# Fewer half-width batches at the end of an attention and soft-MoE kernel, and the last expert's products added to the spreading product

## Chip, cores and metric

One core of a Trainium2 chip runs the whole kernel. The metric is the device time in microseconds, as the median of several runs. The time before the change is 178.54 us (three runs, 178.18 to 178.70).

## What is computed

The reference is attention over 8 batches, 8 heads, 576 positions and 64 dimensions, followed by a mixture of 8 experts with 4 slots each. Heads 0 to 3 see a window of 32 positions, heads 4 to 7 every fourth position of a window of 128.

```python
x = attention(q, k, v)            # 4608 rows of 512
logits = x @ phi                  # 512 x 32 slots
d = softmax(logits, axis=0)       # over the rows
slot_input = (d.T @ x).reshape(8, 4, 512)
for e in range(8):
    h = np.maximum(slot_input[e] @ w1[e], 0.0)     # 512 x 1024
    slot_out[e] = h @ w2[e]                        # 1024 x 512
c = softmax(logits, axis=1)       # over the slots
return c @ slot_out               # 4608 x 512
```

The output is fp32; the kernel computes in fp16 with fp32 sums. The inputs are 62 MB and the output 9.4 MB in HBM.

## The kernel before

**First part.** A software pipeline over the 8 batches (the order of its steps is written out by hand in `ORDER`) computes the attention, the logits and their exponentials `ET`, and sums up the slots' inputs in `U`. All instructions of an engine run in the order in which the program names them (`tc.manual_schedule()`).

**Loads.** POOL issues every load of q, k, v, w1 and w2, with a cast from fp32 to fp16, into one queue that 16 transfer engines work off in order. The loads of the weights are spread between those of the batches. The last ones are issued when the buffers of the last batches come free (line 549 on): `load_full(late, 2, 3, 6)` brings w2 of experts 3, 4 and 5 in one transfer into the tile `late`; then `load_half` brings w2 of experts 6 and 7 in column halves: the left 256 columns of 6 (one transfer) and 7 (two transfers, of four of the eight row chunks each), then the right 256 columns likewise.

**The experts.** After the last batch, the slots' inputs are normalized and transposed (`siTm`), multiplied by w1 (line 608), passed through the ReLU into `h_sb`, transposed (line 618) and copied to `hTm` (lines 620 and 623). `hTm[:, g, c, 32*j : 32*j+32]` holds the hidden values of expert 4g+j for chunk c of the 1,024 hidden units, as 32 columns of which only the four of that expert's slots aren't zero. `emit_so` (line 641) multiplies them by w2 into `so`, a PSUM tile of 128 rows. The products of experts 0 to 3 use the row groups by expert, those of the others by c modulo 4, so four run side by side on the array, and each of the four groups of 32 rows of `so` ends up with a part of the sum.

**Gather and spread.** `gather_so(s)` copies one half (s = 0 left, 1 right; `DH` = 256 columns) of `so` to fp16 on DVE (`so_part`, line 652). `spread_so(s)` multiplies it by a constant matrix `spread`, which adds the four parts and puts the sum into all four groups of 32 rows (`rep`, line 657), and ACT copies that to `so_sb` (line 658).

**Output.** `emit_batch(b, c0, c1)` makes 512 rows of batch b in the columns c0 to c1: four products of `ET` with `so_sb` (line 664, PSUM tiles `f`, four buffers), each scaled and copied to `om[b]` by ACT and DVE in turn (lines 673 and 677), and then one store that POOL issues (line 686; batch 0's left half goes in two stores). The first `NHALF` = 6 batches are made in two passes, left halves first. Between the left halves stand expert 6's right-half products (ahead of batch 2), expert 7's (ahead of batch 4) and the gather of the right half (ahead of batch 5); the spreading of the right half comes behind batch 5. Batches 6 and 7 are made in full width, and the last 64 positions of all batches (`om_l`, line 713) end it.

Of the kernel before, what the change touches and what calls it, by code (L numbers as in the profile page):

```python
# [9 lines left out]
FP32 = mybir.dt.float32  # L10
FP16 = mybir.dt.float16
# [29 lines left out]
DH = DMODEL // 2  # L41
# [55 lines left out]
def kernel(  # L97
# [10 lines left out]
    nc = tc.nc  # L108
# [10 lines left out]
    spread = cst[:, o + 128 : o + 256]  # L119
# [10 lines left out]
    so_part = consts.tile([128, DMODEL], FP16, name="so_part")  # L130
    so_sb = consts.tile([128, DMODEL], FP16, name="so_sb")
    hTm = consts.tile([128, 2, 8, 128], FP16, name="hTm")
# [3 lines left out]
    w1t, w2t = {}, {}  # L136

    def weights_tile(pool, which, e0, e1):
        n = (4 * FDIM, 8 * DMODEL)[which - 1]
        t = pool.tile([128, e1 - e0, n], FP16, name=f"w{which}_{e0}", tag=f"w{which}_{e0}")  # L140
        for e in range(e0, e1):
            of = t[:, e - e0]
            if which == 1:
                w1t[e] = of.rearrange("p (c f) -> p c f", c=4)
            else:
                w2t[e] = of.rearrange("p (c n) -> p c n", c=8)
        return t
# [16 lines left out]
    def slab_weights(e, tag, n):  # L164
        t = fix.tile([128, n], FP16, name=f"w2_{e}", tag=tag)
        w2t[e] = t[:, 0 : 8 * DMODEL].rearrange("p (c n) -> p c n", c=8)
# [9 lines left out]
    ring = ctx.enter_context(tc.tile_pool(name="ring", bufs=2, space=bass.MemoryType.PSUM))  # L176
# [28 lines left out]
    def load_full(t, which, e0, e1):  # L205
        if which == 1:
            nc.gpsimd.dma_start(
                out=t.rearrange("p e (u x) -> p (e u) x", u=2),
                in_=moe_w1[e0:e1].rearrange("e (u p c) f -> p (e u) (c f)", u=2, p=128),
            )  # L210
        else:
            nc.gpsimd.dma_start(
                out=t, in_=moe_w2[e0:e1].rearrange("e (p c) n -> p e (c n)", p=128)
            )

    def load_half(e, s, n):
        src = moe_w2[e].rearrange("(p c) n -> p c n", p=128)
        cols = slice(DH * s, DH * s + DH)
        for u in range(0, 8, n):
            nc.gpsimd.dma_start(out=w2t[e][:, u : u + n, cols], in_=src[:, u : u + n, cols])  # L220
# [249 lines left out]
    for which in "QK":  # L470
        load_raw(which, 1)
    nc.gpsimd.dma_start(
        out=phi_raw.rearrange("p (u c) s -> p u (c s)", u=2),
        in_=moe_phi.rearrange("(u p c) s -> p u (c s)", u=2, c=2),
# [15 lines left out]
    def step(op, b):  # L490
        if op[0] in "ARM" and op[1:] in TILES:
            kind, i = TILES[op[1:]]
            if op[0] == "A":
                tmp[(op[1:], b)] = emit_av(b, kind, i)
            elif op[0] == "R":
                tmp[("R" + op[1:], b)] = emit_recip(b, kind, i, tmp[(op[1:], b)])
            else:
                engine = nc.scalar if op[1:] in ON_ACT else nc.vector
                norm_mult(b, kind, i, tmp.pop((op[1:], b)), tmp.pop(("R" + op[1:], b)), engine)
        elif op in ("S0", "S1", "S2"):  # L500
            tmp[(op, b)] = emit_scores(b, int(op[1]))
        elif op in ("E0", "E1", "E2"):
            emit_exp(b, int(op[1]), tmp.pop(("S" + op[1], b)))
        elif op in ("MK0", "MK1", "MK2"):
            emit_mask(b, int(op[2]))
        elif op[0:2] in ("QT", "KT", "VT"):
            turn(op[0], b, int(op[2]))
        elif op in ("XP0", "XP1"):
            tmp[(op, b)] = xT_plain(b, int(op[2]))
        elif op in ("XD0", "XD1"):  # L510
            tmp[(op, b)] = xT_dil(b, int(op[2]))
        elif op in ("XPc0", "XPc1", "XDc0", "XDc1"):
            xT_copy(b, op[1], int(op[3]), tmp.pop((op[0:2] + op[3], b)))
        elif op in ("VA", "VB", "VC", "VD"):
            tmp[(op, b)] = v_rows(b, "ABCD".index(op[1]))
        elif op in ("VAc", "VBc", "VCc", "VDc"):
            v_place(b, "ABCD".index(op[1]), tmp.pop((op[0:2], b)))
        elif op in ("LG", "EP"):
            tmp[(op, b)] = (back_logits if op == "LG" else back_erow)(b)
        elif op == "ET":  # L520
            back_et(b, tmp.pop(("LG", b)))
        elif op == "ER":
            back_er(b, tmp.pop(("EP", b)))
        else:
            {"ED": back_erd, "U": back_u, "UT": back_add}[op](b)

    def loads(which, b):
        load_raw(which, b)
        if which == "V":
            if b > 2:  # L530
                load_weights(1)
            if b == B - 1:
                load_weights(len(weights))
# [5 lines left out]
    w2b_pool = None  # L539
    for it in range(B + max(s for _, s in STEPS)):  # L540
        for op, stage in STEPS:
            b = it - stage
            if not 0 <= b < B:
                continue
            step(op, b)
            if op in frees and b + 2 < B:
                loads(frees[op], b + 2)
            left.discard((op, b))
            if w2b_pool is None and not left:
                raw_pool.release()  # L550
                w2b_pool = tc.alloc_tile_pool(name="w2b", bufs=1, side="right")
                late = weights_tile(w2b_pool, 2, 3, 6)
                slab_weights(6, "qk0", QK_SLAB)
                slab_weights(7, "qk1", QK_SLAB)
                load_full(late, 2, 3, 6)
                for s in range(2):
                    for e in (6, 7):
                        load_half(e, s, 8 if e == 6 else 4)
        if it == 0:
            nc.vector.tensor_copy(  # L560
                out=phi4, in_=phi_raw[:, :, None, :].broadcast_to([128, 4, 4, N_SLOTS])
            )
# [6 lines left out]
    h_pool = tc.alloc_tile_pool(name="hp", bufs=1)  # L569
# [33 lines left out]
    for fc in range(2):  # L603
        for g in range(2):
            for dc in range(4):
                for j in range(4):
                    e = 4 * g + j
# [4 lines left out]
                        start=(g == 0 and dc == 0),  # L612
                        stop=(g == 1 and dc == 3),
# [3 lines left out]
    for c in range(8):  # L617
# [3 lines left out]
        out=hTm[:, 0].rearrange("p c (j s) -> p c j s", j=4)[:, :, :, 0:16], in_=hT4[:, :, :, 0:16]  # L621
    )
    nc.scalar.copy(
        out=hTm[:, 1].rearrange("p c (j s) -> p c j s", j=4)[:, :, :, 16:32], in_=hT4[:, :, :, 16:32]
    )
    psum_e.release()
    psum_f = tc.alloc_tile_pool(name="psum_f", bufs=4, space=bass.MemoryType.PSUM)

# [6 lines left out]
    def emit_so(s, experts):  # L635
        cols = slice(0, DMODEL) if s is None else slice(DH * s, DH * s + DH)
        for c in range(8):
            for e in experts:
                g, j = divmod(e, 4)
                row = 32 * (j if len(experts) == 4 else c % 4)  # L640
                nc.tensor.matmul(
                    so[row : row + 32, cols],
                    hTm[:, g, c, 32 * j : 32 * j + 32],
                    w2t[e][:, c, cols],
                    start=(e < 4 and c == 0),
                    stop=(e == 7 and c > 3),
                    skip_group_check=True,
                )

    def gather_so(s):  # L650
        cols = slice(DH * s, DH * s + DH)
        nc.vector.tensor_copy(out=so_part[:, cols], in_=so[:, cols])

    def spread_so(s):
        cols = slice(DH * s, DH * s + DH)
        rep = ring.tile([128, DH], FP32, name=f"rep_{s}", tag="ring")
        nc.tensor.matmul(rep, spread, so_part[:, cols], start=True, stop=True)
        nc.scalar.copy(out=so_sb[:, cols], in_=rep)

    turn = [0]  # L660

# [25 lines left out]
                out=dst[:, j0 : j0 + n, c0:c1], in_=om[b][:, j0 : j0 + n, c0:c1]  # L687
            )

    NHALF = 6  # L690
    emit_so(None, (0, 1, 2, 3))
    for e in (4, 5):
        emit_so(None, (e,))
    for e in (6, 7):
        emit_so(0, (e,))
    gather_so(0)
    spread_so(0)
    for b in range(NHALF):
        if b in (2, 4):
            emit_so(1, ({2: 6, 4: 7}[b],))  # L700
        if b == 5:
            gather_so(1)
        emit_batch(b, 0, DH, 2 if b == 0 else 4)
    spread_so(1)
    for b in range(NHALF):
        emit_batch(b, DH, DMODEL)
    for b in range(NHALF, B):
        emit_batch(b, 0, DMODEL)
# [3 lines left out]
    for e in range(2):  # L712
        nc.gpsimd.dma_start(
            out=rest[:, e, 512:576, :].rearrange("n i d -> i n d"), in_=om_l[64 * e : 64 * e + 64]
# [37 lines left out]
```

## Time and profile before

| | |
|---|---|
| profiled execution | 178.29 us |
| its span, first to last instruction | 176.5 us |
| mean granted TensorE clock | 0.87 |
| PE / DVE / ACT / POOL busy | 70% / 71% / 70% / 22% |
| last product, last eviction | 165.0, 165.8 us |
| last output transfer issued, last one landed | 167.0, 175.2 us |

All times within the execution are microseconds from the start of the span. PE is the matrix engine (TensorE), PEld its weight loads, DVE the vector engine, ACT the scalar engine; POOL issues the transfers. In groups and timelines, `L664` is a line of the kernel, `f<-so_sb,ET` says what is written from what, and the brackets say how long the engine was idle before and what ended that. A chain line has a start, a length and the work in it. A window line has its limits and length, the busy time and the number of instructions of PE, PEld, DVE, ACT and POOL, the granted clock, the mean busy share of the 16 transfer engines (over 1 where an engine has two packets under way), and GB/s. A transfer line has the number of issues, the size in KB and the median time from issue to landing. Where the text gives the landing of a single transfer, it is the last of its 16 completion counts in the trace, one from each transfer engine.

### The profile page before, as it was taken

To read this page: it belongs to the slowest core of one execution; us is meant where nothing else is said; L and a number is where in the kernel's file an instruction comes from. 1 tells how busy PE (TensorE), PEld (TensorE's weight loads), DVE (VectorE), ACT (ScalarE), POOL (GpSimd) and SP (SyncE) were. 2 spreads that over 40 slices of the span, in tenths; PEclk is the share of its full clock that TensorE was granted. 3 is DMA by queue.
4 is the path that set the end of the run, shared out by engine and by line. 5 is a ranking of instruction groups with operands and counts; after the bars stand their busy time and mean duration, and the time that the engine had idled before them with its cause. 6 is when DMAs were issued, how large, how long until landed. Compare 5 with 4: busy or idle time off the path is not lost.

```text
span 176.5 us, 4724 instructions
## 1 busy us (share of the span) xinstructions
PE 123.5 (70%) x2004; PEld 80.9 (46%) x2004; DVE 126.0 (71%) x275; ACT 123.5 (70%) x266; POOL 38.4 (22%) x60
## 2 busy tenths in 40 slices
PE   0026928998888888988989888978677295778300
PEld 0015616676566566656766557656332142221000
DVE  6473899999999999999999998465130104878500
ACT  6007758999999999999999999995501104888300
POOL 7321022112112112116000002710000001856600
PEclk9999999969999999999789999996858969655555
DMA  5999999999999999999999999999999999999997
GB/s 83 215 214 210 214 212 215 215 213 214 216 212 217 211 218 215 208 215 220 213 211 217 213 218 216 222 210 225 213 213 221 192 198 175 340 398 397 401 415 209
DMA packets 18981, 40.83 MB, mean 231 GB/s; under 512 B 1169, under 2 KB 11537, under 8 KB 18193
## 3 DMA queue, kind: packets, MB, share of 16 engines
q0 software_dynamic: 18816, 40.41, 113.8%
q8 instruction: 15, 0.25, 0.5%
q1 hardware_dynamic: 144, 0.14, 0.3%
q14 instruction: 6, 0.04, 0.1%
HBM read 62.07 MB, written 9.44 MB: 405 GB/s over the span
## 4 chain that ended last, share of the span: by engine, by line
ACT 38%; DMA 27%; DVE 14%; PE 10%; issue 2%; POOL 2%; POOLq 0%; ACTq 0%
DMA w<-in_moe_w_dram 19%; ACT p L282 10%; DMA phi_raw<-in_moe_phi_dram 8%; ACT vX L253 7%; ACT xp L337 7%; DVE qk L231 5%; PE f L664 5%; ACT om L673 3%; ACT xT L376 3%; ACT xT L378 3%; DVE p L293 3%; DVE vT L231 3%; ACT xd L337 2%; PE s L273 2%; PE rp L357 2%
## 5 line engine op out<-in xcount | busy, mean ns | idle before, releaser
L282 ACT ACTIVATE p<-s 128x1920 f16<-128x1920 f32 (+1 forms) x24 | 44.6, 1857 | 10.2 <-PE s L273 10.1
L273 PE MATMUL s<-qk 32*128 32x128 f16 (+2 forms) x704 | 26.7, 295 | 18.4 <-DVE qk L231 12.0
L253 ACT COPY vX<-rv 128x768 f16<-128x768 f16 (+1 forms) x32 | 27.8, 943 | 1.8 <-PE rv L247 1.8
L316 PEld LDWEIGHTS <-p 128*128 128x128 f16 (+1 forms) x480 | 22.4, 103 | 13.3 <-DVE xp L341 4.0
L337 ACT ACTIVATE xp<-o_P,rc_P 128x64 f16<-128x64 f32 x96 | 26.5, 497 | 2.2 <-DVE rc_P L328 2.2
L273 PEld LDWEIGHTS <-qk 32*128 32x128 f16 x704 | 17.3, 117 | 21.6 <-DVE qk L231 12.0
L293 DVE TENSOR_TENSOR p<-p,masks 128x1920 f16<-128x1920 f16 (+1 forms) x24 | 25.7, 1084 | 0.2
L231 DVE STREAM_TRANSPOSE qk<-rawQ 128x576 uint32<-128x576 uint32 x16 | 18.8, 1243 | 2.7 <-DMA rawQ<-in_q_dram 2.7
L316 PE MATMUL o_P<-vX,p 128*128 128x65 f16 (+1 forms) x288 | 20.0, 205 | 0.8 <-ACT xp L337 0.2
L231 DVE STREAM_TRANSPOSE qk<-rawK 128x576 uint32<-128x576 uint32 x16 | 19.5, 1231 | 0.4 <-DMA rawK<-in_k_dram 0.4
L247 PE MATMUL rv<-cst,vT 128*128 128x128 f16 x176 | 17.5, 242 | 3.2 <-DVE vT L231 1.8
L231 DVE STREAM_TRANSPOSE vT<-rawV 128x576 uint32<-128x576 uint32 x16 | 19.4, 1223 | 0.5 <-DMA rawV<-in_v_dram 0.5
L686 POOL DMA_DIRECT2D out_dram<-om x15 | 11.1, 744 | 39.2 <-DVE om L677 34.8
L247 PEld LDWEIGHTS <-vT 128*128 128x128 f16 x176 | 13.2, 124 | 7.5 <-issue 3.7
L677 DVE TENSOR_SCALAR om<-f,rrow 128x256 f16<-128x256 f32 (+1 forms) x28 | 13.5, 519 | 3.5 <-PE f L664 2.9
L664 PE MATMUL f<-so_sb,ET 32*128 32x256 f16 (+1 forms) x60 | 12.5, 392 | 3.9 <-ACT om L673 2.7
L673 ACT ACTIVATE om<-f,rrow 128x256 f16<-128x256 f32 (+1 forms) x28 | 12.8, 503 | 2.6 <-PE f L664 2.0
L376 ACT COPY xT<-rp 128x576 f16<-128x576 f16 x16 | 11.5, 909 | 1.3 <-PE rp L357 1.3
L316 PE MATMUL o_D<-vX,p 128*128 128x65 f16 x128 | 9.9, 202 | 2.5 <-DVE xp L341 2.0
L201 POOL DMA_DIRECT2D rawQ<-in_q_dram x8 | 5.1, 633 | 29.4 <-DVE rc_P L328 18.4
L378 ACT COPY xT<-rd 128x576 f16<-128x576 f16 x16 | 10.6, 795 | 0.0
L341 DVE TENSOR_TENSOR xd<-o_D,rc_D 128x256 f16<-128x256 f32 x24 | 9.9, 412 | 0.2
(81 smaller groups left out, 176.7 us busy)
## 6 DMA issues: line engine op xcount, KB each, us to landing
w<-in_moe_w_dram POOLq DMA_DIRECT2D x3, 3072.0 KB, 35.5
out_dram<-om POOLq DMA_DIRECT2D x11, 512.0 KB, 4.6
w<-in_moe_w_dram POOLq DMA_DIRECT2D x5, 1024.0 KB, 15.9
rawQ<-in_q_dram POOLq DMA_DIRECT2D x8, 576.0 KB, 12.7
rawK<-in_k_dram POOLq DMA_DIRECT2D x8, 576.0 KB, 11.4
rawV<-in_v_dram POOLq DMA_DIRECT2D x8, 576.0 KB, 11.6
out_dram<-om POOLq DMA_DIRECT2D x2, 1024.0 KB, 7.3
w<-in_moe_w_dram POOLq DMA_DIRECT2D x2, 512.0 KB, 36.7
```

The costliest lines, as they stand in the source:

```text
L231: nc.vector.transpose(out=out_, in_=in_)
L247: nc.tensor.transpose(rg[:, n_t, :, c, :], rows, ident)
L253: copy(out=vX[b % 2][:, t0 : t0 + n, :, 0:D], in_=rg.rearrange("p n h c d -> p n h (c d)"))
L273: nc.tensor.matmul(sps[:, h, c0 : c0 + w], kk, qq, start=(tt == 0), stop=(tt == 1))
L282: return nc.scalar.activation(out=pt, in_=sps[:, :, 0:n], func=AF.Exp, scale=SCALE)
L293: return nc.vector.tensor_tensor(out=pt, in0=pt, in1=m, op=ALU.mult)
L316: nc.tensor.matmul(o[rows, h, :], lhs, rhs, start=(n == 0), stop=(n == len(jobs) - 1), skip_group_check=True,)
L337: nc.scalar.activation(out=dst[:, h], in_=src[:, h], func=AF.Copy, scale=rc[:, h : h + 1])
L376: copy(out=xT_t[b][:, c, :], in_=rg[:, 0:S])
L378: copy(out=xT_t[b][:, 2 + c, :].rearrange("p (i r) -> p i r", r=DIL), in_=rg[:, :, 0:SUB].rearrange("p r i -> p i r"),)
L664: nc.tensor.matmul(fp[:, 0 : c1 - c0], ET[32 * j : 32 * j + 32, m : m + 128], so_sb[32 * j : 32 * j + 32, c0:c1], start=True, stop=True,)
L673: nc.scalar.activation(out=dst, in_=fp[:, 0 : c1 - c0], func=AF.Copy, scale=rrow[:, blk : blk + 1])
```

## The change

- `NHALF` is 4 instead of 6: batches 4 and 5 are made and stored in full width.
- Expert 7's products leave `so`. Its hidden values are copied on DVE into a new tile `hT7`, repeated four times side by side, and its products are 128 wide: they give the same 32 rows in all four groups. They are added in PSUM to the spreading product: `gather_so` now starts that product (`stop=False`) as soon as experts 0 to 6 are gathered, and `last_so` adds expert 7's eight products and copies the result to `so_sb`.
- Right half: expert 6's products, the gather and the spreading product stand ahead of batch 2, and `last_so(1)` behind batch 3.
- w2 of expert 3 gets its own tile and its own transfer, ahead of that of experts 4 and 5.

```diff
-                late = weights_tile(w2b_pool, 2, 3, 6)
+                late = {x: weights_tile(w2b_pool, 2, *x) for x in ((3, 4), (4, 6))}
 ...
-                load_full(late, 2, 3, 6)
+                for x, t in late.items():
+                    load_full(t, 2, *x)
 ...
+    hT7 = h_pool.tile([128, 8, 4, 32], FP16, name="hT7", tag="hT7")
+    nc.vector.tensor_copy(out=hT7, in_=hTm[:, 1, :, None, 96:128].broadcast_to([128, 8, 4, 32]))
 ...
-                    stop=(e == 7 and c > 3),
+                    stop=(e == 6 and c > 3),
 ...
+    rep = {}
     def gather_so(s):
         cols = slice(DH * s, DH * s + DH)
         nc.vector.tensor_copy(out=so_part[:, cols], in_=so[:, cols])
+        rep[s] = ring.tile([128, DH], FP32, name=f"rep_{s}", tag="ring")
+        nc.tensor.matmul(rep[s], spread, so_part[:, cols], start=True, stop=False)
 
-    def spread_so(s):
+    def last_so(s):
         cols = slice(DH * s, DH * s + DH)
-        rep = ring.tile([128, DH], FP32, name=f"rep_{s}", tag="ring")
-        nc.tensor.matmul(rep, spread, so_part[:, cols], start=True, stop=True)
-        nc.scalar.copy(out=so_sb[:, cols], in_=rep)
+        for c in range(8):
+            nc.tensor.matmul(
+                rep[s],
+                hT7[:, c].rearrange("p a s -> p (a s)"),
+                w2t[7][:, c, cols],
+                start=False,
+                stop=(c == 7),
+            )
+        nc.scalar.copy(out=so_sb[:, cols], in_=rep[s])
 ...
-    NHALF = 6
+    NHALF = 4
     emit_so(None, (0, 1, 2, 3))
     for e in (4, 5):
         emit_so(None, (e,))
-    for e in (6, 7):
-        emit_so(0, (e,))
+    emit_so(0, (6,))
     gather_so(0)
-    spread_so(0)
+    last_so(0)
     for b in range(NHALF):
-        if b in (2, 4):
-            emit_so(1, ({2: 6, 4: 7}[b],))
-        if b == 5:
+        if b == 2:
+            emit_so(1, (6,))
             gather_so(1)
         emit_batch(b, 0, DH, 2 if b == 0 else 4)
-    spread_so(1)
+        if b == 3:
+            last_so(1)
```

## The prediction

> **What bounds the kernel now.** I read the page's slices first, then the chain of waits, then the last 40 us: queue, engines, transfers.
>
> Page, part 2 (40 slices of 4.4 us):
>
> ```profile
> PEclk9999999969999999999789999996858969655555
> DMA  5999999999999999999999999999999999999997
> GB/s 83 215 214 210 214 212 215 215 213 214 216 212 217 211 218 215 208 215 220 213 211 217 213 218 216 222 210 225 213 213 221 192 198 175 340 398 397 401 415 209
> ```
>
> The transfer engines are busy from end to end: inputs at some 213 GB/s of fp16 landed, outputs at 400 GB/s of fp32. The dip to 175 GB/s is where loads end and outputs begin. The chain of waits, there:
>
> ```profile
> 112.33 34.05 DMA w<-in_moe_w_dram
> ...
> 146.76 0.43 DVE so_part L652
> 147.23 0.28 PE rep L657
> 147.54 0.38 ACT so_sb L658
> 147.96 0.31 PE f L664 x4
> ...
> 154.63 0.41 PE f L664 x4
> ```
>
> From the landing of expert 7's left half (146.37) to the first product of the output (147.96) lie 1.59 us of small steps; the right half's output products begin at 154.63. The chain leaves out that the transfer queue, one queue issued by POOL, drains until 175.2 while the engines are done at 165.8. In windows:
>
> ```profile
> 148.50:149.50 1.00, 0.71 (x8) 0.29 (x9) 1.00 (x3) 1.00 (x4) 0.10 (x1) 1.00 1.15 155
> 149.50:150.50 1.00, 0.89 (x13) 0.38 (x13) 0.79 (x3) 0.80 (x3) 1.00 (x2) 1.00 0.70 94
> 152.50:154.50 2.00, 1.16 (x6) 0.45 (x5) 1.96 (x5) 1.90 (x5) 1.29 (x2) 0.50 1.98 405
> 168.00:170.00 2.00, 0.00 (x0) 0.00 (x0) 0.00 (x0) 0.00 (x0) 0.00 (x0) 0.50 1.46 411
> ```
>
> The last two columns are DMA share and GB/s. There is a hole at 149 to 150.5, but not in every transfer engine: the 16 completions of the last load come between 149.0 and 151.70. The early engines wait for output, the latest goes straight on (its first output completes at 152.45). All 16 then write at one pace, and the latest at the loads' end is still about 0.6 us late at the end. So **the end is the latest engine's load end, 151.70, plus its output work, plus a tail**, as long as output is ready for it. POOL's issues and the transfers:
>
> ```profile
> 149.40 3.03 POOL L686 DMA_DIRECT2D out_dram<-om  x4 [33.97 <-DVE om L677]
> 155.06 0.75 POOL L686 DMA_DIRECT2D out_dram<-om  x1 [0.37 <-issue]
> 156.48 0.74 POOL L686 DMA_DIRECT2D out_dram<-om  x1 [0.67 <-ACT om L673]
> ...
> out_dram<-om POOLq DMA_DIRECT2D x11, 512.0 KB, 4.6
> out_dram<-om POOLq DMA_DIRECT2D x2, 1024.0 KB, 7.3
> out_dram<-om POOLq DMA_DIRECT2D x2, 256.0 KB, 3.0
> ```
>
> The issue at 149.40 has its first packet at 150.68: 1.28 us. Eleven half-width batches (512 KB) land from 153.14 to 167.69, 1.323 us each; the two full batches (1 MB) land at 170.18 and 172.73, 2.52 us each. The issue at 156.48 is the first right half; its landing, 161.06, less its own 1.32, less 0.3 that a landing lies behind its last packet, says that the queue came to it at 159.45. It could have started at 156.48 + 1.28 = 157.76: **1.7 us of slack**, worked out from these, not shown as a wait.
>
> **The change part by part.**
>
> *Two batches full instead of halved.* Four transfers of 1.323 become two of 2.52: 5.29 - 5.04 = **-0.25 us**, all on the queue that sets the end. Sixteen half-width evictions become eight full ones (0.47 against 0.69 us each on ACT): off the path, as the engines end 9 us before the queue.
>
> *w2 of expert 3 alone.* One more issue on POOL, 0.77 us, ahead of expert 6's at 106.34; the issues behind it wait until 111.58 anyway for a buffer, and land 30 us later. Hidden; without that backlog 0.77. On the queue it adds one completion: two 256 KB pieces land 0.69 apart, one 512 KB piece 1.32, so 2 x 0.69 - 1.32 = **+0.06**. What it lets go early:
>
> ```profile
> 138.44 0.40 PE L641 MATMUL so<-w,hTm 128*32 128x512 f16 x3 [0.52 <-DVE hTm L620]
> 141.15 4.61 PE L641 MATMUL so<-w,hTm 128*32 128x512 f16 x57 [2.31 <-DMA w<-in_moe_w_dram]
> ```
>
> Experts 0 to 3 (32 products) no longer wait for 141.15. They end by about 140.3, but nothing can end before expert 7 lands at 146.37; today PE is through with the rest at 145.76. Worth nothing by itself.
>
> *The copy to hT7.* 1,024 values a partition on DVE behind ACT's copy that ends at 139.0. The 512-value copy at L620 takes 0.42, so 0.4 to 0.9. DVE is idle until 146.76: nothing; without that cover, at most 0.9.
>
> *Expert 7, left half.* Gather (0.43), spreading (0.28) and their gaps leave the path behind the landing; in come four of eight 128-wide products (the first four have their weights at 145.04). Products of 512 columns start 0.213 apart at clock 1.0 and 0.427 at 0.5, so one of 256 costs 0.107 or 0.213, and four end at 147.0, or at 147.46 at half clock, against 147.50 for the spreading now. Output products begin 0.46 or 0.04 earlier. Which? Clock 1.0 in 144.3 to 151.1 follows a stretch (140.9 to 144.3) in which PE worked off the late experts 0 to 5. With 0 to 3 done earlier, that stretch holds some 1.1 us of work at full clock. I take half clock, 0.04. The Trainium skill, "TensorE: Matmul & The Clock Gate", Part 1, says that the array's clock is released by a busy window of about 3.4 us and falls back after an idle one; by that rule spending the products early speaks against this change. The trace bears it out in kind: the 3.4 us after the wait for 141.15 ran at 0.5. In either case the latest transfer engine gains nothing from an earlier first output, since it isn't waiting at 151.70.
>
> *Right half.* This is where it can cost. Now expert 6's and 7's products are slipped between batches 1/2 and 3/4, and the gather between batches 4/5. ACT's evictions:
>
> ```profile
> 148.26 1.67 ACT L673 ACTIVATE om<-f,rrow 128x256 f16<-128x256 f32 x4 [0.35 <-PE f L664]
> 150.13 1.72 ACT L673 ACTIVATE om<-f,rrow 128x256 f16<-128x256 f32 x4 [0.20 <-PE f L664]
> 152.51 1.77 ACT L673 ACTIVATE om<-f,rrow 128x256 f16<-128x256 f32 x4 [0.66 <-PE f L664]
> 155.04 5.62 ACT L673 ACTIVATE om<-f,rrow 128x256 f16<-128x256 f32 x12 [0.46 <-PE f L664]
> ```
>
> After the change: (a) the gather stands ahead of batch 2 on DVE, and the spreading on PE waits for it with batch 2's output products behind it. DVE is free of batch 1 at 150.03, gathers until 150.45, the spreading starts at 150.5, batch 2's first product ends at 150.9: ACT resumes at 150.94 where it resumed at 150.13, +0.8. (b) Batches 2 and 3 take 1.75 more: to 152.7. (c) PE starts the eight wide products at 152.05 (batch 3's last output product); at the clock of 0.5 that the trace shows there they take 8 x 0.213 = 1.7 us plus 0.15 to drain: 153.95. Expert 7's last quarter lands at 151.70, before its turn. Then the copy to so_sb, 0.37, and the first right-half product at 154.42. Today that is 154.63: **only 0.2 earlier, with two half batches (2.65 us of queue) fewer ahead of it**. So the slack of 1.7 becomes 1.7 + 0.2 - 2.65 = -0.75: the queue runs dry for **0.75 us**, even for its latest engine, just before the first right half. Bounds: at full clock in (c) and the 0.46 of earlier start, the slack stays positive: 0. With batches 0 to 2 at half clock as well (0.2 to 0.3 more) and no gain in (c): 1.0; if the next two right halves too come late (they have 0.35 us to spare, and today one of the gaps between issues there is 1.42), up to 2.0. I take 0.75, nearest to the rows. Behind it the queue gains on nothing: each later issue comes 0.95 to 1.45 after the last, for 1.32 of work, and full batches (1.5 of evictions for 2.52 of queue) rebuild the lead. Where the queue is dry for all engines, the 0.06 of the split is swallowed.
>
> **Sum**: -0.25 + 0.75 = +0.50 us. On the profiled execution (span 176.5, 1.79 around it, 178.29) 178.79; the median of the runs is 178.54, 0.25 above it, so **179.0 us**. That is 0.28%, at the edge of the 0.3% that a measurement of this kernel can tell from no change.
>
> **Rivals.** *A: the queue never runs dry* (not slower). The wide products run at clock 1.0, or the two bubbles overlap evictions more than I allow; it decides when the first right half is issued before 155.6. Then only -0.25 + 0.06 is left: 178.35. For: 1.7 us of slack today, and half of the loss hangs on a clock that changed seven times after 120. Against: f products alone never kept the clock at 1.0 after 151.1.
>
> *B: the queue runs dry longer*, 1.2 to 2.0 us, with several right halves late one after the other: +1 to +1.75, about 179.9. For: POOL's issues come 0.53 us behind the last eviction and 1.28 before the first packet, so nothing is regained quickly. Against: ACT and DVE need 0.95 per half batch, the queue 1.32.
>
> *C: each transfer holds the queue for a fixed time.* A 256 KB output takes 3.0 us from issue to landing, 0.69 of it its own bytes. If the remaining 2.3 were paid in series, one transfer fewer (two outputs out, one load in) would give -2.3 -0.25: 176.0. The pace of 1.32 us for queued 512 KB speaks against it. The Trainium skill, "DMA: Bandwidth & Descriptors", Anatomy of one DMA, has such a form, about 2 us plus bytes at 436 GB/s per transfer; by it one fewer would be an estimated 2 us less. The trace doesn't agree for queued ones: the fixed part is 0.06.
>
> *D: the transfer engines share a rate*, so that an earlier first output helps even the latest: -0.46 -0.25, 177.85. Against: packets take 76 to 80 ns whether half of the engines write or all.
>
> **How the numbers follow.** Forecast (dry 0.4 to 1.1 us, 178.6 to 179.4): 0.44. A 0.22, B 0.23, C 0.02, D 0.06, other 0.03. Over 0.3% is 0.54 us: the forecast's case is split, 0.24 slower and 0.20 within; A is within but for 0.03 faster; B is slower; C and D faster; the rest is halved. Faster 0.12, within 0.39, slower 0.49. The range leaves out C, half of D and the end of B: 178.0 to 180.1.
>
> **What would show it.** Right: the windows near 156 to 158 show the DMA share below 1.9; the eight wide products take 1.7 us; the first right half is issued near 156.2; full batches land 2.5 us apart; no change before 138. Wrong: DMA share at 1.9 or more through to 165 (A); a second hole (B); load completions that end elsewhere than near 151.7, which I have no term for.

## The result and the profile after

The changed kernel takes 179.77 us (median of 6 runs, 179.38 to 180.11) against 178.29 us for the kernel before in the same runs: **1.48 us slower, ratio 1.0080, 95% interval 1.0062 to 1.0098**. Its profiled execution takes 179.70 us, its span 177.9 us, 1.4 longer. Page, part 2:

```profile
PEclk9999999998599999999889999996858985555555
DMA  5999999999999999999999999999999999999998
GB/s 94 205 213 216 209 213 216 216 213 218 217 210 213 215 216 212 213 215 215 215 214 212 219 214 215 230 212 210 225 214 206 197 197 186 340 276 406 411 414 229
```

Up to the output the queue's slices are much as before; the last load lands at 151.45 (151.70 before). New is the slice of 276 GB/s between 340 and 406, where the transfer queue should be writing at 400. The windows of the changed kernel (DMA share and GB/s last):

```profile
153.00:154.00 1.00, 1.00 (x7) 0.63 (x5) 0.09 (x1) 0.00 (x1) 0.81 (x2) 0.50 0.79 154
156.60:157.90 1.30, 1.03 (x5) 0.30 (x5) 0.93 (x3) 1.21 (x4) 1.01 (x2) 0.50 0.06 7
```

**The queue runs dry twice**: ahead of batch 2's left half, where the early transfer engines stop from 153.2 on and all of them stand from 153.8 to 154.0, and ahead of the first right half, where all stand from 156.8 to 158.0. POOL's timeline of the changed kernel (start, length, what; in brackets the idle time before):

```profile
149.17 2.17 POOL L700 DMA_DIRECT2D out_dram<-om  x3 [21.95 <-DVE om L691]
152.67 0.75 POOL L700 DMA_DIRECT2D out_dram<-om  x1 [1.33 <-ACT om L687]
153.62 0.74 POOL L700 DMA_DIRECT2D out_dram<-om  x1 [0.19 <-issue]
156.69 0.74 POOL L700 DMA_DIRECT2D out_dram<-om  x1 [2.33 <-ACT om L687]
```

And PE's:

```profile
139.50 2.86 PE L644 MATMUL so<-w,hTm 128*32 128x512 f16 x48 [0.52 <-DVE hTm L621]
...
150.50 0.37 PE L660 MATMUL rep<-so_part,cst 128*128 128x256 f16 x1 [0.53 <-DVE so_part L657]
...
152.50 1.89 PE L665 MATMUL rep<-w,hT 128*128 128x256 f16 x8
154.84 0.40 PE L678 MATMUL f<-so_sb,ET 32*128 32x256 f16 x4 [0.46 <-ACT so_sb L672]
```

The products of experts 0 to 5 now run in one piece, without the wait until 141.15. Batch 2's left half is issued at 152.67 (151.69 before): its output products stood on PE behind the spreading product, which waited for the gather until 150.50. The first right half is issued 3.07 us after the last left half (153.62 to 156.69), where it was 1.42 before (155.06 to 156.48). Between them lie the eight wide products, 1.89 us, in which ACT has nothing to evict, as its timeline shows (idle 1.42):

```profile
151.23 1.77 ACT L687 ACTIVATE om<-f,rrow 128x256 f16<-128x256 f32 x4 [1.37 <-PE f L678]
154.42 0.37 ACT L672 CAST so_sb<-rep 128x256 f16<-128x256 f32 x1 [1.42 <-PE rep L665]
155.25 3.69 ACT L687 ACTIVATE om<-f,rrow 128x256 f16<-128x256 f32 x8 [0.46 <-PE f L678]
```

The account of the latest transfer engine, from its completion counts (after less before): -0.25 at the end of the loads; +0.45 at batch 2's left half, which completes 1.8 us after batch 1's instead of 1.35; +1.55 at the first right half, which completes 2.85 us after the transfer ahead of it instead of 1.3; -0.3 in the rest, most of it behind that, with two more batches in full rows. Sum +1.5. The second hole costs the queue some 0.3 more than the 1.2 in which no engine moves anything. Most of this is that the engines don't all stop and start at once: the DMA share is 0.51, 0.00, 0.00 and 1.79 in the four half microseconds from 156.5 to 158.5, against about 2.0 when the queue runs, so the mean engine loses 1.4.

### The profile page after: what moved, and what is told of

It is laid out like the page before. It is cut to its first block, busy times and chain, and to the rows that moved or that the text cites. A ratio compares the mean times of both kernels' runs of the same rounds, so it can differ in the third digit from the quotient of the medians.

```text
span 177.9 us, 4697 instructions
## 1 busy us (share of the span) xinstructions
PE 126.5 (71%) x1996; PEld 83.6 (47%) x1996; DVE 125.8 (71%) x272; ACT 123.2 (69%) x262; POOL 37.5 (21%) x59
## 4 chain that ended last, share of the span: by engine, by line
ACT 31%; DMA 26%; DVE 17%; PE 16%; issue 2%; POOL 2%; POOLq 0%
DMA w<-in_moe_w_dram 18%; ACT p L282 10%; DMA phi_raw<-in_moe_phi_dram 8%; ACT xp L337 6%; DVE qk L231 5%; ACT vX L253 5%; PE f L678 4%; PE s L273 3%; ACT xT L378 3%; DVE p L293 3%; DVE vT L231 3%; ACT xT L376 2%; PE rep L665 2%; ACT om L687 2%; DVE om L691 2%
## 5 line engine op out<-in xcount | busy, mean ns | idle before, releaser
L282 ACT ACTIVATE p<-s 128x1920 f16<-128x1920 f32 (+1 forms) x24 | 43.1, 1797 | 10.1 <-PE s L273 10.0
L316 PEld LDWEIGHTS <-p 128*128 128x128 f16 (+1 forms) x480 | 23.3, 105 | 13.4 <-DVE xp L341 4.4
L253 ACT COPY vX<-rv 128x768 f16<-128x768 f16 (+1 forms) x32 | 26.4, 888 | 1.7 <-PE rv L247 1.7
L337 ACT ACTIVATE xp<-o_P,rc_P 128x64 f16<-128x64 f32 x96 | 25.4, 451 | 2.8 <-DVE rc_P L328 2.8
L247 PE MATMUL rv<-cst,vT 128*128 128x128 f16 x176 | 18.9, 255 | 3.1 <-DVE vT L231 1.8
L691 DVE TENSOR_SCALAR om<-f,rrow 128x256 f16<-128x256 f32 (+1 forms) x24 | 12.8, 569 | 7.8 <-PE f L678 7.3
L247 PEld LDWEIGHTS <-vT 128*128 128x128 f16 x176 | 14.0, 128 | 7.5 <-issue 3.8
L700 POOL DMA_DIRECT2D out_dram<-om x13 | 9.6, 742 | 30.4 <-DVE om L691 24.7
L687 ACT ACTIVATE om<-f,rrow 128x256 f16<-128x256 f32 (+1 forms) x24 | 12.0, 543 | 3.3 <-PE f L678 2.6
L376 ACT COPY xT<-rp 128x576 f16<-128x576 f16 x16 | 10.8, 818 | 1.6 <-PE rp L357 1.6
```

What stands on the lines that cost most here:

```text
L247: nc.tensor.transpose(rg[:, n_t, :, c, :], rows, ident)
L253: copy(out=vX[b % 2][:, t0 : t0 + n, :, 0:D], in_=rg.rearrange("p n h c d -> p n h (c d)"))
L282: return nc.scalar.activation(out=pt, in_=sps[:, :, 0:n], func=AF.Exp, scale=SCALE)
L316: nc.tensor.matmul(o[rows, h, :], lhs, rhs, start=(n == 0), stop=(n == len(jobs) - 1), skip_group_check=True,)
L337: nc.scalar.activation(out=dst[:, h], in_=src[:, h], func=AF.Copy, scale=rc[:, h : h + 1])
L687: nc.scalar.activation(out=dst, in_=fp[:, 0 : c1 - c0], func=AF.Copy, scale=rrow[:, blk : blk + 1])
```

## The experiments

The differences below are worked out from the ratio to the kernel before in the same runs (178.3 to 178.6 us); the interval of the ratio stands beside them. Windows, issues and clocks are those of one profiled execution each, and the end of the loads varies between 151.45 and 152.26 from one to the next.

**1. Six halves again, everything else as changed.**

```diff
-    NHALF = 4
+    NHALF = 6
 ...
-        if b == 3:
+        if b == 5:
             last_so(1)
```

> The changed kernel with six half-width batches again, and the right half's wide products (last_so(1)) behind the sixth left half instead of the fourth; the rest as changed. Theory (the transfer queue runs dry because four left halves, with the wide right-half products and their gather among them, are issued faster than their successors): the hole at 156.6 to 158.0 goes, since two more half batches (2.65 us of queue) lie in front of the first right half; what is left is the shorter hole at 153.2 to 154.0 that the early gather makes. 178.5 to 179.0, against 179.8 as changed and 178.3 before. Rival (the wide products, hT7 or the split load cost by themselves, whatever is queued): 179.6 to 179.8, and the DMA share stays high.

179.92 us, ratio 1.0087 (1.0074 to 1.0100), +1.55: as slow as with four. My theory failed here. POOL's timeline of this run, the first right half last:

```profile
156.07 0.75 POOL L700 DMA_DIRECT2D out_dram<-om  x1 [0.21 <-issue]
159.14 0.75 POOL L700 DMA_DIRECT2D out_dram<-om  x1 [2.33 <-ACT om L687]
```

PE's, and below it a window:

```profile
154.95 1.89 PE L665 MATMUL rep<-w,hT 128*128 128x256 f16 x8
```

```profile
159.40:160.40 1.00, 0.83 (x5) 0.20 (x4) 0.63 (x2) 0.91 (x3) 0.81 (x2) 0.50 0.01 0
```

The window's last columns are DMA share and GB/s. The same 3.07 us between the last left half and the first right half, and the queue is dry from 159.5 to 160.5. Two half batches more hold the queue for 2.65 us, but they are issued 2.38 us after the ones before (153.69 to 156.07): they lengthen the lead by 0.27 us only, about what two batches in halves cost against full rows. So the number of halves is nearly neutral, and the length of what stands between left and right decides.

**2. Four halves with the last expert as before.**

```diff
-    NHALF = 6
+    NHALF = 4
 ...
-        if b in (2, 4):
-            emit_so(1, ({2: 6, 4: 7}[b],))
-        if b == 5:
+        if b in (2, 3):
+            emit_so(1, ({2: 6, 3: 7}[b],))
+        if b == 3:
             gather_so(1)
```

> The kernel before with NHALF 4: expert 7's right-half products (32 wide, as before) and the gather ahead of batch 3, the spreading behind it; no hT7, no split load. Theory (it is the 1.8 us of wide products at half clock, with nothing else to evict, that four halves can't cover): the first right half is issued near 155.6 and is there about when the queue needs it, hole 0 to 0.3; 178.0 to 178.6. Rival (two half batches fewer are by themselves too few, however the last expert is done): a hole of 0.7 to 1.4 us, 178.9 to 179.5.

178.36 us, ratio 0.9995 (0.9986 to 1.0004): no difference, as the theory had it, and the converse of run 1. Two short holes (the longer at 155.1 to 155.5, ahead of batch 3, whose products stand behind the wait for expert 7's load) eat up what the full rows give in the profiled execution, which at 178.79 us is the slowest of the twelve. Last left half and first right half are 1.55 us apart, in POOL's timeline:

```profile
154.24 0.74 POOL L686 DMA_DIRECT2D out_dram<-om  x1 [1.21 <-ACT so_sb L658]
155.79 0.74 POOL L686 DMA_DIRECT2D out_dram<-om  x1 [0.81 <-ACT om L673]
```

**3. The split load alone**, the kernel before with `late` in two tiles and two transfers, as in the change.

> The kernel before with w2 of expert 3 in a transfer of its own, and nothing else of the change. Theory: 178.2 to 178.5, no difference beyond 0.15 us: the products of experts 0 to 3 start at 138.4 instead of after 141, but the landing of expert 7 sets what follows. Rival (an extra transfer costs, or the cooler PE clock after it does): 178.7 to 179.0.

178.37 us, ratio 1.0002 (0.9991 to 1.0013): nothing. The added transfer costs the queue too little to be seen.

**4. The changed kernel with one transfer for experts 3 to 5**, the same lines taken back.

> The changed kernel with w2 of experts 3, 4 and 5 in one transfer again. Theory with the clock in it (the products of experts 0 to 3 done early leave PE idle just before 145, and the granted clock stays at 0.5 from 145.3 on, which makes the wide products slow on both halves): without the split the clock is 1.0 in about 144 to 151 as before, the first output comes 0.3 to 0.5 us earlier, and the hole ahead of the first right half shrinks by as much: 179.2 to 179.5. Rival (the split doesn't matter): 179.7 to 179.9.

179.66 us, ratio 1.0086 (1.0056 to 1.0116): the rival's time. The profile says why my gain didn't come: the clock was 1.0 from 146.4 to 153.2, but the products of experts 0 to 5 waited until 141.11 and ran at 0.5 from there to 146.4, and the first output product came at 148.77 instead of 147.69. One thing made up for the other. The theory asked for a clock of 1.0 from 144 on; that didn't come, so this run doesn't decide on it. It shows the four left halves at clock 1.0, though, in PE's and ACT's timelines:

```profile
148.77 0.29 PE L677 MATMUL f<-so_sb,ET 32*128 32x256 f16 x4 [0.46 <-ACT so_sb L671]
152.89 1.64 PE L664 MATMUL rep<-w,hT 128*128 128x256 f16 x8
151.73 1.67 ACT L686 ACTIVATE om<-f,rrow 128x256 f16<-128x256 f32 x4 [0.99 <-PE f L677]
```

From the first output product to the first of the right half's wide products it takes 4.12 us here and 4.81 as changed (147.69 to 152.50), and ACT waits 0.99 ahead of batch 2 instead of 1.37.

**5. Right half as before, left half as changed.**

```diff
         if b == 2:
             emit_so(1, (6,))
-            gather_so(1)
 ...
         if b == 3:
-            last_so(1)
+            emit_so(1, (7,))
+            spread_narrow(1)    # gather, spreading product, copy to so_sb
```

> The changed kernel (four halves, split load, left half with the wide products) with only the right half as before: expert 6's products ahead of batch 2, then behind batch 3 expert 7's 32-wide products, the gather and the spreading. Theory after the first four runs (the right half's wide products and its early gather are what the queue waits for, with four halves as with six): both holes close but for some 0.2 us, and the two full-width batches pay their 0.25: 178.0 to 178.4. Rival (the left half's wide products or hT7 cost as well): 178.8 to 179.8.

178.76 us, ratio 1.0013 (1.0000 to 1.0026): +0.23: most of the loss is gone, but the median lies in neither range, just below the rival's 178.8. In the windows of this run the first hole is gone and the second shorter:

```profile
153.00:154.00 1.00, 0.37 (x1) 0.10 (x1) 0.41 (x1) 0.13 (x1) 0.81 (x2) 0.50 1.98 402
156.60:157.50 0.90, 0.73 (x6) 0.14 (x6) 0.51 (x2) 0.82 (x2) 0.70 (x2) 0.50 0.21 40
```

The products, the gather and the spreading stand one behind the other here (last left half at 153.44, first right half at 156.13, 2.69 apart), while run 2 has the gather beside batch 3's products.

**6. Left half as before, right half as changed**: the mirror image.

> The mirror image: the changed kernel with the left half as before (expert 7's 32-wide products into so, gather, spreading) and the right half with the early gather and the wide products. Theory: both holes stay, 179.6 to 180.2, as the earlier start of the left half is worth little. Rival (the left half is what costs): 178.2 to 178.8.

180.09 us, ratio 1.0089 (1.0070 to 1.0108): +1.6, the whole loss. Runs 5 and 6 place it in the right half.

**7. The right half's wide products doubled**, by eight products of zeros.

```diff
+        for c in range(8 * s):
+            nc.tensor.matmul(rep[s], zero7, w2t[7][:, c, cols], start=False, stop=False)
```

> The changed kernel with eight more wide products in the right half, of a tile of zeros with w2 of expert 7, added to the same sum. Theory: nothing covers them, so the second hole grows by their 1.7 us at a granted clock of 0.5: 181.2 to 181.7. Rival (there is slack left in the queue, or the products aren't what the queue waits for): below 180.6.

181.24 us, ratio 1.0157 (1.0136 to 1.0179): +2.80, as the theory had it.

**8. Half of the right half's wide products.**

```diff
-        for c in range(8):
+        for c in range(4 * s, 8):
```

> The changed kernel with only four of the eight wide products in the right half (chunks 0 to 3 of expert 7 are left out of the right 256 columns). Theory: 0.85 us less before the first right half at a granted clock of 0.5, so the second hole shrinks from 1.4 to 0.5 us: 178.8 to 179.2. Rival (the hole has another last cause, the gather or the early issue of four halves): 179.5 to 180.0.

179.28 us, ratio 1.0044 (1.0030 to 1.0059): +0.79, within 0.1 us of the range foreseen. With 4, 8 and 16 products the loss is 0.79, 1.43 and 2.80 us: 0.16 to 0.17 us for each. The distance from the issue of the last left half to that of the first right half shows it without the left halves, which ran partly at clock 1.0 in run 7: 2.22, 3.07 and 4.78 us (153.86 to 156.08 here, 153.27 to 158.05 in run 7), 0.21 us for each product, which is what one takes at half clock. What PE spends there delays the first right half in full.

**9. The spreading product behind batch 3's products.**

```diff
         if b == 2:
             emit_so(1, (6,))
+        if b == 3:
             gather_so(1)        # now the copy alone
         emit_batch(b, 0, DH, 2 if b == 0 else 4)
         if b == 3:
+            start_rep(1)        # the spreading product
             last_so(1)
```

> The changed kernel, all eight wide products, but the right half's gather ahead of batch 3 instead of batch 2, and its spreading product behind batch 3's products, so that no output product of batches 2 and 3 is queued on PE behind a wait for the gather. Theory: the first hole goes, batches 2 and 3 are evicted some 0.8 us earlier, the wide products start as much earlier and the second hole shrinks to about 0.5: 178.5 to 178.9. Rival (only the wide products' length counts, and the steps before them merely change places): 179.5 to 179.9.

179.36 us, ratio 1.0055 (1.0037 to 1.0073): +0.98, 0.45 less than as changed, where I had expected some 0.9 less; it lies between theory and rival. Batch 2 is issued at 151.67, a full microsecond earlier, and the first hole is gone. But the first right half comes only 0.8 us earlier, still 3.13 behind the last left half (POOL's timeline):

```profile
152.78 0.75 POOL L702 DMA_DIRECT2D out_dram<-om  x1 [0.36 <-issue]
155.91 0.75 POOL L702 DMA_DIRECT2D out_dram<-om  x1 [2.38 <-ACT om L689]
```

By the medians the wait for the gather is thus about a third of the loss and the wide products the rest. The share is rough: the intervals of the two kernels (1.0062 to 1.0098 and 1.0037 to 1.0073) overlap.

**10. PE kept busy, first form.** Idle 128-wide products into a spare PSUM tile, ahead of experts 6 and 7, during the gathers, and one behind each output product of the left halves.

```diff
+        keep_warm(2, 512)       # in gather_so, ahead of the spreading product
 ...
+                if warm:            # in emit_batch, for the left halves
+                    keep_warm(1, 256)
 ...
+    keep_warm(6, 512)           # nobody reads them
     emit_so(0, (6,))
     gather_so(0)
+    keep_warm(2, 512)
     last_so(0)
+    keep_warm(4, 512)
```

> The changed kernel with idle stretches of PE between 142 and 152 filled with 128-wide products into a spare PSUM tile that nobody reads. If the granted clock then is 1.0 until past 153, the right half's wide products take 1.0 us instead of 1.9 and the small steps before them some 0.1 us less each. Theory with the clock as part of the cause: the second hole shrinks from 1.4 to about 0.4 us, 178.5 to 179.1. Rival (the order of the steps alone makes the holes): 179.6 to 180.0, even at clock 1.0. If the clock doesn't rise, it tells nothing.

183.90 us, ratio 1.0302 (1.0264 to 1.0341): inconclusive for the question. The clock was 1.0 to 160.3 and the wide products took 1.04 us, but each output product with its idle one took 0.425 us, so that four took 1.7 us instead of 0.95, and the queue ran dry ahead of every left half from batch 2 on.

**11. PE kept busy, second form**: 19 idle products, none within a batch.

> The changed kernel with 19 idle products of 512 columns into a spare PSUM tile, put only where PE waits anyway: ahead of expert 6's products, during both gathers, ahead of the first output product, and behind batches 0 and 2; none between the output products of a batch, where they cost more than they gave. If the granted clock is 1.0 until 153 or later: the right half's wide products take 1.0 instead of 1.9 us, and the theory says 178.7 to 179.2 with a second hole of about 0.5. Rival (the clock has no part in it): 179.6 to 180.0 in spite of clock 1.0.

179.47 us, ratio 1.0065 (1.0041 to 1.0090): between the two. Clock 1.0 from 146.3 to 156.5, and the wide products do take the shorter time, in PE's timeline:

```profile
152.72 1.05 PE L679 MATMUL rep<-w,hT 128*128 128x256 f16 x8
```

Last left half to first right half is 2.13 us. The queues of the same run (packets, MB, share):

```profile
q8 instruction: 16, 0.26, 0.5%
```

This line tells what took part of the gain away: 16 fetches of instructions where every other run but number 10 has 15. The sixteenth, at 162.5, falls among the stores, and one of the 16 transfer engines completes the next store 1.1 us behind the next latest and never catches up: the last store completes between 175.6 and 176.0 on 15 of them and at 177.0 on this one. Without it this execution, at 180.10 us slower than the median, would have ended about 1 us earlier, within the theory's range; that is worked out, not tried, and whether the other five executions lose the same isn't shown.

**12. Five halves, the last expert as before.**

```diff
-    NHALF = 6
+    NHALF = 5
 ...
-        if b == 5:
+        if b == 4:
             gather_so(1)
```

> The kernel before with five halves instead of six and the gather of the right half ahead of batch 4; nothing else. Theory: the slack of 1.7 us ahead of the first right half pays for one half batch less (it loses some 0.4), no hole, and one batch in full rows gains 0.12: 178.2 to 178.5 where before has 178.4. Rival (any step down from six opens a hole): 178.8 or more.

178.27 us, ratio 0.9991 (0.9980 to 1.0002): 0.16 us less by its median, no hole, as foreseen; the interval still takes in no difference. It is the best version of the study, but not shown to beat the kernel before.

## Why the prediction was right, and where not

**The bound.** That the end is the latest engine's load end plus its output work, as long as output is there for it, held where there is no hole: the runs without one (3 and 12) lose nothing, and their last transfer lands 23.7 and 23.75 us after the last load (23.5 before). Where the queue runs dry ahead of the first right half, wholly or (runs 2 and 11) in part, the issue of that half takes the place of the loads' end, and the profiles follow it closely:

| kernel | first right half issued | last transfer lands | apart |
|---|---|---|---|
| as changed | 156.69 | 176.70 | 20.01 |
| run 2 | 155.79 | 175.79 | 20.00 |
| run 4 | 156.84 | 176.85 | 20.01 |
| run 5 | 156.13 | 176.13 | 20.00 |
| run 6 | 157.03 | 177.05 | 20.02 |
| run 7 | 158.05 | 178.05 | 20.00 |
| run 8 | 156.08 | 176.08 | 20.00 |
| run 9 | 155.91 | 175.90 | 19.99 |
| run 10 (a fetch of 1.35 us among the stores) | 158.97 | 180.30 | 21.33 |
| run 11 (a fetch of 0.99 us among the stores) | 155.97 | 177.03 | 21.06 |
| six halves, dry queue: run 1 | 159.14 | 176.86 | 17.72 |
| six halves, before | 156.48 | 175.23 | 18.75 |

With four halves the end comes 20.0 us after that issue, whatever stood ahead of it, and the sixteenth fetch is paid on top. So the first hole costs nothing by itself, only through what it does to that issue: run 9 has none, and the same 20.0. Nor does an earlier first output help (rival D): the last completion of the first store comes 0.65 to 0.80 us after the end of the loads in all runs but run 4, whether that store was issued at 149.06 (run 7) or at 149.99 (run 11). Rival C (a fixed time for each transfer) fell with run 3, where one transfer more made no difference.

**The direction.** The queue runs dry ahead of the first right half, as the prediction had it, with the shares falling below 1.9 between 156 and 158, the wide products at 1.89 us (1.85 foreseen) and the full batches some 2.6 us apart. It had named a second hole as a sign for rival B; there is one, but it lies ahead of the other, at batch 2's left half.

**The size: +0.50 foreseen, +1.48 measured.** The term that failed is the 0.75 us of dry queue. It was 1.2, beyond the 0.4 to 1.1 of the forecast's own case, and 1.5 by what the landings lose. The time stayed within the range because the range was drawn wide enough for rival B. In the terms of the table, the prediction has the first right half issued 0.2 earlier than before, 2.65 - 0.25 = 2.40 us more work of the queue behind it, and 1.7 of slack: -0.2 + 2.40 - 1.7 = +0.50. The profiles have it issued 0.2 later, 20.0 - 17.7 = 2.3 more work behind it, and 18.75 - 17.72 = 1.0 of slack: +1.5.

- **The slack was 1.0, not 1.7**, as far as the one run with six halves and a dry queue tells. The prediction let a store on an idle queue land 1.28 + 1.32 + 0.3 = 2.9 us after its issue. The first right half landed 3.37 after it as changed (156.69 to 160.06) and 3.42 in run 1 (159.14 to 162.56); with 3.4 in place of 2.9 the working gives a slack of 1.2. Of the three terms the 0.3 is one too small: the last landing before lies 0.40 behind the last packet (174.83 to 175.23).
- **The issue came 0.4 to 0.5 later than foreseen, by the clock.** I took the clock as 1.0 in batches 0 to 2; it was 0.5 from 145.3 on. From the first output product to the wide products the prediction has 4.13 us (147.92 to 152.05); run 4, at clock 1.0, took 4.12, and the changed kernel 4.81. I had priced that at 0.2 to 0.3 and kept it for the bound. Step (a), the gather's wait, is part of it: +0.8 foreseen, +0.8 in run 4 (ACT idles 0.99 there, 0.20 before), +1.2 as changed (1.37). An earlier left half (147.69 instead of 147.92) gave 0.2 back; the first right-half product came at 154.84 instead of 154.42.
- I followed step (a) to the first right half alone. It makes batch 2 late as well, 0.45 on the latest engine; by the table that adds nothing to the end, as the queue would have stood dry for longer instead.
- -0.25 for full rows: -0.2 behind the first right half.

**The attribution.** The sum treats the two half batches fewer as 2.65 us of queue lost, and the bubbles as a small change of date. Run 1 shows it the other way round: with the two half batches back the loss stays, since they bring 0.27 us of lead and no more, and runs 2 and 12 lose nothing with fewer of them. In the sum that was hidden, because each half batch that left took its 0.9 to 1.2 us of eviction along. Rival B (dry for 1.2 to 2.0 us) came nearest in size, but its mechanism, one right half after the other late, isn't what happened: from 158.5 to 163 the DMA share is 1.94 or more.

**The clock.** The Trainium skill, "TensorE: Matmul & The Clock Gate", Part 1, calls the window in which PE's activity is measured free-running, about 3.4 us long. The traces agree: the changes lie 3.4 us or a multiple apart, and at other times in each run (145.3 as changed, 144.2 in run 1, 143.3 and 150.1 in run 7, 146.4 and 153.2 in run 4). So the price of the wide products, 1.05 or 1.89 us, can't be read from the clock of the trace before. Whether doing the products of experts 0 to 3 early takes clock away later stays open: run 3 does them early and loses nothing, and in run 4, which doesn't, the changes of the clock fall at other times.

## What to carry to other kernels

Where a queue of stores sets the end, look first whether it runs dry, and ahead of which store: from there on the issue of that store, and not the end of the loads, sets the end. Then follow each edit to the issue times and compare two distances: how far apart transfers are issued, and how long the queue holds each. Work that no eviction can cover, such as a product in whose shadow the evicting engines stand idle, then costs its full length once the slack is used up, and putting more transfers in front of it helps only by the difference of these two, not by their length. A product that shortens the path behind a landing is worth nothing while the queue is still busy with loads, as on the left half here.

## What the runs showed of the hardware

- Fetches of instructions set single transfer engines back. One of 16 KB takes 0.9 to 1.1 us in the traces (1.35 in run 10). In the changed kernel the 16 completions of a load lie within 0.20 us ahead of the first fetch (at 22.25); of the next load, 15 lie within 0.16 and one comes 1.24 behind the first. By the end of the loads the spread is 2.4 to 2.7 us in the profiles of before and after, with the counts in groups about 1.1 us apart, so the fetches make most of it; that is argued from these steps. All 15 fall among the loads here. The two runs with 38 or more added PE instructions (10 and 11) have a sixteenth, among the stores.
- With one transfer more, POOL waited for an old one. In the changed kernel the last load is issued at 126.48:

```profile
126.48 0.74 POOL L220 DMA_DIRECT2D w<-in_moe_w_dram  x1 [10.69 <-DMA w<-in_moe_w_dram]
```

It uses the completion semaphore of the transfer issued eight before it, which landed at 126.19; before, it was issued at 114.67. It cost nothing, as the queue was 25 us behind.
- From issue to the first packet of a store on an idle queue it took 1.3 us (149.40 to 150.68 before, 156.69 to 158.0 after), to the last of its 16 completions 3.4 us with 512 KB, and POOL started about 0.5 us behind the last eviction.
